# Three raw buffers for late weights, six buffers for reads of h, and the first pair's low parts of q and k on VectorE

## The chip, the cores and the metric

The kernel runs on one core of a Trainium2 chip. The time is what the device takes for one execution, in microseconds (us). A core has five engines that run their own instructions in a fixed order and meet at semaphores: TensorE (PE in the profile; PEld is its weight load), VectorE (DVE), ScalarE (ACT), GpSimd (POOL) and SyncE (SP). An engine that waits holds up everything behind it in its order. "SPq" and "ACTq" are the queues from which SP and ACT issue DMAs.

## What is computed

Three stages follow each other, all in float32:

```python
# attention with decay: q, k, v (4, 8, 576, 64), f (4, 8, 576)
cum = cumsum(log(clip(f, 1e-4, 1.0)))
scores = q @ k.T / 8 + cum[:, None] - cum[None, :]     # causal
x = softmax(scores) @ v                                # -> (2304, 512)
# first feed-forward: w_in (512, 2048), w_out (2048, 512)
h = x @ w_in
y = (h * tanh(softplus(h))) @ w_out                    # "Mish" of h
# second feed-forward: w1, w2, w3 (512, 768), w_out (768, 512)
out = max(y @ w1, y @ w2, y @ w3) @ w_out
```

## The kernel before

**Split operands.** Each float32 operand of a large product is split into a high part, which is the value rounded to the type that TensorE multiplies, and a low part, the rest. `split` does that with a copy and a subtraction, each on an engine that the caller names. `mm3` (L182 to L184) multiplies high by high, high by low and low by high: three matmuls for each product.

**Late weights.** The inputs' weights lie in HBM as 64-bit numbers. `load_f32` reads a chunk of them as raw pairs of 32-bit words (tile `wr`, L155) and builds the float32 value with five instructions: L160 (or L158 on ACT), L161, L164, L167 and L171, the rest on VectorE. Then `load_split` has the value split on two engines; for all late weights that is GpSimd twice (the copy at L139 and the subtraction at L143). "Late" are the weights that are loaded after attention: `load_w_out` (moe_w_out, 16 chunks of 512 columns, two raw buffers `wr`) and `load_w2` (24 chunks of 384 columns of w1, w2 and w3, then 6 chunks of 512 of the last w_out, one raw buffer `wr1`). The pool `stg2` holds the raw tiles and two buffers of the value `wt`.

**The stages in order.** Attention runs over 16 pairs of heads; `load` reads a pair's q, k, v and running sums, and `prep` splits and transposes them. The splits there are made by `split_raw`, the high part on VectorE and the low part on GpSimd. Between the pairs, `h_steps` computes `h` for blocks of 256 tokens; ACT or VectorE copies each result out of PSUM (tile `he`, L539 or L542) and a DMA writes it to HBM. What is left of the h steps after attention, "the tail of the h stage", runs from about 410 to 497 us, with `load_w_out` beside it.

Then comes the y stage, up to about 715 us. Its loop has one step for each pair of 128 rows of w_out and each block of 512 tokens (the last block has 256), 12 matmuls of 512 columns to a step. `load_g` reads h (tile `g`, L631), ACT applies Mish (L634) and makes the high part `gh` (L137), and VectorE subtracts to get the low part `gl` (L143). It is called three steps ahead, with four buffers each for `g`, `gh` and `gl`. Every second step also draws one chunk from `load_w2`. After the last step of a block the four results `y` are copied out of PSUM (tile `ze`, four buffers; L661 on VectorE, L664 on ACT) and written to HBM as `z_d`. The last stage (products `g` and `o`) reads them again as `yr`.

**What sets the order.** The order of each engine's instructions is written when the kernel is compiled, by a planner that simulates the engines and takes the ready instruction with the best priority. `tc.high_priority(AHEAD)` moves the reads and splits of h ahead of the rest. A tile with more buffers lets the planner put the next writer of that tile earlier.

Of the kernel before, what the change touches and what calls it, by code (L numbers as in the profile page):

```python
# [9 lines left out]
F32 = mybir.dt.float32  # L10
F32R = mybir.dt.float32r
BF16 = mybir.dt.bfloat16
I32 = mybir.dt.int32
# [18 lines left out]
AHEAD = 3000  # L32
BLK = 256
BLK2 = 512
# [33 lines left out]
def tile_decay_attention__mish_ff__max3_ff(  # L68
# [66 lines left out]
    def split(dst_hi, dst_lo, src, eng_hi, eng_lo):  # L135
        if eng_hi == "act":
            nc.scalar.activation(dst_hi, src, AF.Copy)  # L137
        elif eng_hi == "pool":
            nc.gpsimd.tensor_scalar(dst_hi, src, 1.0, 1.0, op0=ALU.mult, op1=ALU.mult)  # L139
        else:  # L140
            nc.vector.tensor_copy(dst_hi, src)
        eng = nc.gpsimd if eng_lo == "pool" else nc.vector
        eng.tensor_tensor(out=dst_lo, in0=src, in1=dst_hi, op=ALU.subtract)  # L143
# [3 lines left out]
    def load_f32(pool, srcs, bufs=None, abs_eng="dve", raw="wr"):  # L147

        m, n = len(srcs), srcs[0].shape[1]
        t = pool.tile([128, m, n], F32, name="wt", tag="wt", bufs=bufs)  # L150
        r = pool.tile([128, m, n, 2], I32, name=raw, tag=raw, bufs=bufs if raw == "wr" else 1)

        with tc.issue_after(pace[-1].ins) if pace else ExitStack():
            for i, src in enumerate(srcs):
                nc.sync.dma_start(r[:, i].rearrange("p n w -> p (n w)"), src.bitcast(I32))  # L155
        lo, hi, ti = r[:, :, :, 0], r[:, :, :, 1], t.bitcast(I32)
        if abs_eng == "act":
            nc.scalar.activation(t, hi.bitcast(F32), AF.Abs)  # L158
        else:
            nc.vector.tensor_scalar(ti, hi, 0x7FFFFFFF, None, op0=ALU.bitwise_and)  # L160
        nc.vector.tensor_scalar(  # L161
            t, t, F32_MIN_AS_HIGH_HALF, F32_MAX_AS_HIGH_HALF, op0=ALU.max, op1=ALU.min
        )
        nc.vector.tensor_scalar(  # L164
            ti, ti, 3, 0x3FFFFFF8, op0=ALU.logical_shift_left, op1=ALU.bitwise_and
        )
        nc.vector.scalar_tensor_tensor(  # L167
            out=ti, in0=hi, scalar=-0x40000000, in1=ti,
            op0=ALU.bitwise_and, op1=ALU.bitwise_or,
        )  # L170
        nc.vector.scalar_tensor_tensor(  # L171
            out=ti, in0=lo, scalar=29, in1=ti,
            op0=ALU.logical_shift_right, op1=ALU.bitwise_or,
        )
        return t
# [14 lines left out]
    wst = sa.enter_context(tc.tile_pool(name="wst", bufs=2))  # L190
# [55 lines left out]
    count = dict(pair=0, prep=0, unit=0)  # L246
# [20 lines left out]
                src[b, hs, 512:S, :].rearrange("h p d -> p h d"),  # L267
            )

    def split_raw(t, r, eng="dve"):  # L270

        split(t[:, :, 0], t[:, :, 1], r.rearrange("p (n d) -> p n d", d=64), eng, "pool")

    def load(b, hp):

# [33 lines left out]
    def prep(J):  # L309

        qh = as_.tile([128, 2, 512], F32R, name="qh", bufs=2)
        ql = as_.tile([128, 2, 512], F32R, name="ql", bufs=2)
        kk = as_.tile([128, 2, S], F32R, name="kT", bufs=2)
        last = q4[count["prep"] % 2]
        count["prep"] += 1

        def turn(dst, c, src):
            nc.tensor.transpose(dst[:, c:c + 128].bitcast(F32R), src, identr)

        rest = att_psum("tr")  # L320

        split_raw(qk[1], raw[1])
        split_raw(qk[0], raw[0])
        nc.gpsimd.tensor_scalar(
            qk[0][:, :, 2], raw[0].rearrange("p (n d) -> p n d", d=64), 1.0, 1.0, op0=ALU.mult, op1=ALU.mult
        )
        for i, part, dst, n in ((1, 0, kk, 0), (0, 0, qh, 1), (0, 1, ql, 2)):
            src = lambda blk: qk[i][:, blk, part:part + 2, :].rearrange("p a d -> p (a d)")
            for h in range(2):
                tr = att_psum("tr")  # L330
                for c in range(4):
                    turn(tr, c * 128, src(4 * h + c))
                nc.scalar.activation(
                    dst[:, h, 0:512].rearrange("p (c t) -> p c t", t=4),
                    tr.rearrange("p (t c) -> p c t", t=4),
                    AF.Copy,
                )
            turn(rest, n * 128, src(8))
        rr = rest[:, 0:384].rearrange("p (i h c) -> p i h c", i=3, h=2)
        nc.scalar.activation(kk[:, :, 512:S], rr[:, 0], AF.Copy)  # L340
        for a in range(2):
            nc.scalar.activation(
                last[:, a].rearrange("p (a c) -> p a c", c=64)[:, 0:4:3, :], rr[:, 1 + a], AF.Copy
            )
        split_raw(J["vs"], raw[2], "act")
        c2, c4 = J["cb"]
        for n, src, dst in ((2, 0, 5), (1, 3, 2), (1, 4, 4)):
            nc.gpsimd.affine_select(
                out=c2[:, :, dst:dst + n, :], in_=c2[:, :, src:src + n, :], pattern=[[0, 2], [0, n], [-1, 128]],
                compare_op=ALU.is_ge, fill=-1e30, base=0, channel_multiplier=1,  # L350
            )
        nc.gpsimd.tensor_tensor(out=c4[:, 512:S], in0=c4[:, 512:S], in1=mask4, op=ALU.add)
        J.update(q=(qh, ql), q4=last, k=kk)
# [222 lines left out]
    wo = [wop.tile([128, 2, 2, DM], F32R, name=f"wo{fp}") for fp in range(NFP)]  # L576
    stg2 = sb.enter_context(tc.tile_pool(name="stg2", bufs=2, side="right", reuse_waits="tile"))
    gp_ = sb.enter_context(tc.tile_pool(name="gp", bufs=4, side="right", reuse_waits="tile"))
    zst = sb.enter_context(tc.tile_pool(name="zst", bufs=4, side="right", reuse_waits="tile"))
    yps = sb.enter_context(tc.tile_pool(name="yps", bufs=5, space=PSUM, side="right", reuse_waits="tile"))  # L580

    def load_w_out():
# [23 lines left out]
    def load_w2():  # L606
        for c in range(KD):
            for m in range(3):
                src = (moe2_w1, moe2_w2, moe2_w3)[m][c * 128:(c + 1) * 128, :]
                for d in range(0, DFF2, 384):  # L610
                    ds = slice(d, d + 384)
                    load_split(
                        stg2, wm[m][:, 0, c:c + 1, ds], wm[m][:, 1, c:c + 1, ds], [src[:, ds]],
                        "pool", "pool", raw="wr1",
                    )
                    yield
        for c in range(NF2):
            load_split(
                stg2, wo2[:, 0, c:c + 1, :], wo2[:, 1, c:c + 1, :],
                [moe2_w_out[c * 128:(c + 1) * 128, :]], "pool", "pool", raw="wr1",  # L620
            )
            yield

    def load_g(ib, fp, a):

        g = gp_.tile([128, BLK2], F32, name="g")
        gh = gp_.tile([128, BLK2], F32R, name="gh")
        gl = gp_.tile([128, BLK2], F32R, name="gl")
        n = blocks1[ib][1]
        if n == BLK2:  # L630
            nc.sync.dma_start(g, h_d[ib][fp][:, a, :])  # L631
        else:
            nc.sync.dma_start(g.rearrange("p (a n) -> p a n", a=2), h_d[ib][fp][:])
        nc.scalar.activation(g, g, AF.Mish)  # L634
        split(gh, gl, g, "act", "dve")
        return [(t, (gh[:, i * n:(i + 1) * n], gl[:, i * n:(i + 1) * n])) for i, t in enumerate([a] if n == BLK2 else [0, 1])]

    wgen3 = load_w2()
    todo = [(ib, fp, a) for ib, (_, n) in enumerate(blocks1) for fp in range(NFP) for a in range(n // BLK)]
    with tc.high_priority(AHEAD):  # L640
        ahead = [load_g(*t) for t in todo[:3]]
    for step, (ib, fp, a) in enumerate(todo):
        n = blocks1[ib][1]
        if fp == 0 and a == 0:
            y = [yps.tile([128, n], F32, name=f"y{j}", tag="y") for j in range(KD)]
        parts = ahead.pop(0)
        if step + 3 < len(todo):
            with tc.high_priority(AHEAD):
                ahead.append(load_g(*todo[step + 3]))
        for t, g in parts:  # L650
            final = fp == NFP - 1 and t == 1
            for j in range(KD):
                js = slice(j * 128, (j + 1) * 128)
                mm3(y[j], (wo[fp][:, 0, t, js], wo[fp][:, 1, t, js]), g, fp == 0 and t == 0, final)
        if step % 2:
            next(wgen3, None)
        if final:
            for j in range(KD):
                ze = zst.tile([128, n], F32, name="ze", tag="ze")
                if j % 2:  # L660
                    nc.vector.tensor_copy(ze, y[j])  # L661
                    nc.sync.dma_start(z_d[ib][:, j, :], ze)
                else:
                    nc.scalar.activation(ze, y[j], AF.Copy)  # L664
                    nc.scalar.dma_start(z_d[ib][:, j, :], ze)
            if ib == 0:
                nc.sync.dma_start(y0[0], z_d[0][:, :, 0:BLK])
                split(y0[1], y0[2], y0[0], "act", "pool")
# [81 lines left out]
```

## Time and profile before

| what | value |
|---|---|
| median of 3 runs | 1026.43 us (1024.89 to 1028.39) |
| the profiled execution | 1024.48 us |
| its span, first to last instruction | 1022.5 us |
| mean granted TensorE clock | 0.968 |
| busy: PE, DVE, ACT, POOL | 955.2, 511.9, 422.0, 378.3 us |

The profile shows one execution. Busy time of PE includes matmuls that wait inside the engine, since their ends are modelled; counts of matmuls in a stretch of time tell more. A granted clock of 1.00 is 2.4 GHz, 0.5 is 1.2 GHz.

### The profile page before, as it was taken

How to read it: one execution, taken by the hardware profiler on the slowest of the kernel's cores; microseconds unless marked ns; L12 is line 12 of the kernel's file. 1: busy time of each engine (PE TensorE's matmuls, PEld its weight loads, DVE VectorE, ACT ScalarE, POOL GpSimd, SP SyncE). 2: the span in 40 equal slices, each digit the busy share in tenths (PEclk: the TensorE clock that was granted, in tenths of full speed). 3: DMA queues.
4: the chain of work that ended last, by engine and by line, in shares of the span. 5: the costliest groups of instructions: out<-in, count | busy, mean ns of one | idle time of the engine just before them, and what ended most of it. 6: DMA issues, size and time to landing. Idle time of an engine off the chain costs nothing.

```text
span 1022.5 us, 15879 instructions
## 1 busy us (share of the span) xinstructions
PE 955.2 (93%) x5756; PEld 840.6 (82%) x5756; DVE 511.9 (50%) x1159; ACT 422.0 (41%) x920; POOL 378.3 (37%) x437
## 2 busy tenths in 40 slices
PE   4886799999998999998898999999999999999998
PEld 4675689999998999998776777778988888888886
DVE  4868898656556556479645655653211112011110
ACT  4876667666667565421233434332211211211111
POOL 6756875566447521445423423230111111011110
PEclk9987789999999999999898999999999999999999
DMA  6545646545344412765445554552300100200101
GB/s 151 143 141 161 172 131 207 151 145 159 109 143 131 138 57 89 268 208 187 143 144 177 160 185 149 190 172 75 104 21 1 62 21 1 83 1 2 40 0 42
DMA packets 105294, 119.16 MB, mean 117 GB/s; under 512 B 33856, under 2 KB 77376, under 8 KB 105216
## 3 DMA queue, kind: packets, MB, share of 16 engines
q1 hardware_dynamic: 92288, 103.73, 33.0%
q10 hardware_dynamic: 12928, 14.42, 4.0%
q8 instruction: 45, 0.74, 0.3%
q14 instruction: 33, 0.27, 0.1%
HBM read 85.01 MB, written 33.10 MB: 116 GB/s over the span
## 4 chain that ended last, share of the span: by engine, by line
PE 57%; DMA 18%; DVE 17%; issue 2%; ACT 2%; SPq 2%; POOL 1%; DVEq 0%; ACTq 0%; POOLq 0%
PE g L183 7%; PE g L184 7%; PE g L182 7%; DMA wr<-in_moe_w_dram 7%; DMA wr<-in_moe_w_out_dram 5%; PE h L183 4%; PE h L184 4%; PE h L182 4%; PE av L451 4%; PE sc L363 4%; DVE wt L171 3%; PE pp L438 3%; DVE wt L167 3%; PE o L182 2%; PE o L184 2%; PE o L183 2%
## 5 line engine op out<-in xcount | busy, mean ns | idle before, releaser
L182 PE MATMUL h<-xh,wi 128*128 128x256 f32 x576 | 167.4, 292 | 8.2 <-ACT he L542 6.7
L183 PE MATMUL h<-xl,wi 128*128 128x256 f32 x576 | 167.1, 290 | 1.9 <-POOL xl L143 1.9
L184 PE MATMUL h<-xh,wi 128*128 128x256 f32 x576 | 166.2, 289 | 0.0
L143 POOL TENSOR_TENSOR hl<-mx,hh 128x512 fp32r<-128x512 f32 x27 | 36.5, 1350 | 271.3 <-ACT hh L137 271.3
L182 PE MATMUL g<-yh,wm 128*128 128x512 f32 (+1 forms) x360 | 134.5, 374 | 0.0
L183 PE MATMUL g<-yl,wm 128*128 128x512 f32 (+1 forms) x360 | 134.5, 374 | 0.0
L184 PE MATMUL g<-yh,wm 128*128 128x512 f32 (+1 forms) x360 | 134.5, 374 | 0.0
L183 PE MATMUL y<-gl,wo 128*128 128x512 f32 (+1 forms) x320 | 121.6, 380 | 10.5 <-DVE gl L143 10.5
L182 PE MATMUL y<-gh,wo 128*128 128x512 f32 (+1 forms) x320 | 120.5, 378 | 4.6 <-ACT gh L137 3.4
L182 PEld LDWEIGHTS h<-xh,wi 128*128 128x128 f32 x576 | 111.9, 195 | 9.5 <-ACT he L542 7.0
L184 PE MATMUL y<-gh,wo 128*128 128x512 f32 (+1 forms) x320 | 119.5, 375 | 0.0
L183 PEld LDWEIGHTS h<-xl,wi 128*128 128x128 f32 x576 | 111.9, 194 | 3.2 <-POOL xl L143 2.4
L184 PEld LDWEIGHTS h<-xh,wi 128*128 128x128 f32 x576 | 111.8, 194 | 0.3
L634 ACT ACTIVATE g<-g 128x512 f32<-128x512 f32 x72 | 45.5, 632 | 138.5 <-DMA g<-h_d 128.3
L706 DVE TENSOR_TENSOR mx<-g,mx 128x512 f32<-128x512 f32 x27 | 18.7, 691 | 158.6 <-PE g L184 158.6
L183 PEld LDWEIGHTS y<-gl,wo 128*128 128x128 f32 x320 | 61.8, 193 | 26.5 <-DVE gl L143 17.0
L414 ACT ACTIVATE P<-P,mn 128x128 f32<-128x128 f32 (+3 forms) x128 | 70.9, 556 | 27.3 <-DVE mn L408 26.4
L183 PEld LDWEIGHTS g<-yl,wm 128*128 128x128 f32 x360 | 68.2, 189 | 13.4
L184 PEld LDWEIGHTS g<-yh,wm 128*128 128x128 f32 x360 | 68.2, 189 | 13.2
L182 PEld LDWEIGHTS g<-yh,wm 128*128 128x128 f32 x360 | 68.1, 189 | 13.2
L182 PEld LDWEIGHTS y<-gh,wo 128*128 128x128 f32 x320 | 62.0, 194 | 17.3 <-ACT gh L137 4.9
L438 PE MATMUL pp<-ident,P 128*128 128x128 f32 x320 | 64.4, 303 | 11.9 <-POOL P L388 11.7
(101 smaller groups left out, 1989.9 us busy)
## 6 DMA issues: line engine op xcount, KB each, us to landing
g<-h_d SPq DMA_DIRECT2D x72, 256.0 KB, 3.3
h_d<-he ACTq DMA_DIRECT2D x46, 256.0 KB, 2.9
wr<-in_moe_w_out_dram SPq DMA_DIRECT2D x22, 512.0 KB, 4.0
wr<-in_moe_w_dram SPq DMA_DIRECT2D x24, 384.0 KB, 3.4
cb<-cum_d SPq DMA_DIRECT2D x64, 128.0 KB, 3.4
wr<-in_moe_w_in_dram SPq DMA_DIRECT2D x32, 256.0 KB, 3.3
h_d<-he SPq DMA_DIRECT2D x26, 256.0 KB, 3.2
cb<-cum_d SPq DMA_DIRECT2D x32, 144.0 KB, 3.3
```

Of the source, the lines that this page charges most:

```text
L143: eng.tensor_tensor(out=dst_lo, in0=src, in1=dst_hi, op=ALU.subtract)
L167: nc.vector.scalar_tensor_tensor(out=ti, in0=hi, scalar=-0x40000000, in1=ti, op0=ALU.bitwise_and, op1=ALU.bitwise_or,)
L171: nc.vector.scalar_tensor_tensor(out=ti, in0=lo, scalar=29, in1=ti, op0=ALU.logical_shift_right, op1=ALU.bitwise_or,)
L182: nc.tensor.matmul(ps, wh, xh, start=start, stop=False, skip_group_check=True)
L183: nc.tensor.matmul(ps, wh, xl, start=False, stop=False, skip_group_check=True)
L184: nc.tensor.matmul(ps, wl, xh, start=False, stop=stop, skip_group_check=True)
L363: nc.tensor.matmul(o, lhs, rhs, start=n == 0, stop=n == len(mms) - 1, skip_group_check=True)
L414: nc.scalar.activation(Pt, Pt, AF.Exp, scale=-1.0, bias=mn[:, col - 1:col], accum_out=sm[:, ci:ci + 1],)
L438: nc.tensor.transpose(pp[:, n * 128:n * 128 + 128], Pt[:, k0:k0 + 128], ident)
L451: nc.tensor.matmul(avp[h][:, off:off + w], vl, T[:, i, c:c + w], start=kt == 0 and i == 0 and not (g == 0 and h == 1), stop=last and i == ...
L634: nc.scalar.activation(g, g, AF.Mish)
L706: nc.vector.tensor_tensor(out=mx, in0=g[1], in1=mx, op=ALU.max)
```

## The change

The raw tile gets three buffers wherever the pool is not the early one (`wst`), and `load_w2` uses the same raw tile as `load_w_out`, so both share three buffers. `load_g` is cut in two: `load_g` reads h and applies Mish, five steps ahead and with six buffers; `split_g` makes the high and low parts, two steps ahead and with three buffers each. The tile `ze` goes from four buffers to three. In the first call of `prep`, the low parts of q and k are subtracted on VectorE and no longer on GpSimd.

```diff
-        r = pool.tile([128, m, n, 2], I32, name=raw, tag=raw, bufs=bufs if raw == "wr" else 1)
+        r = pool.tile([128, m, n, 2], I32, name=raw, tag=raw, bufs=3 if pool is not wst else bufs)
...
-    def split_raw(t, r, eng="dve"):
+    def split_raw(t, r, eng="dve", eng_lo="pool"):
-        split(t[:, :, 0], t[:, :, 1], r.rearrange("p (n d) -> p n d", d=64), eng, "pool")
+        split(t[:, :, 0], t[:, :, 1], r.rearrange("p (n d) -> p n d", d=64), eng, eng_lo)
...
-        split_raw(qk[1], raw[1])
-        split_raw(qk[0], raw[0])
+        first = "dve" if count["prep"] == 1 else "pool"
+        split_raw(qk[1], raw[1], "dve", first)
+        split_raw(qk[0], raw[0], "dve", first)
...
-    zst = sb.enter_context(tc.tile_pool(name="zst", bufs=4, side="right", reuse_waits="tile"))
+    zst = sb.enter_context(tc.tile_pool(name="zst", bufs=3, side="right", reuse_waits="tile"))
...
-                        "pool", "pool", raw="wr1",
+                        "pool", "pool",
...
-                [moe2_w_out[c * 128:(c + 1) * 128, :]], "pool", "pool", raw="wr1",
+                [moe2_w_out[c * 128:(c + 1) * 128, :]], "pool", "pool",
...
-        g = gp_.tile([128, BLK2], F32, name="g")
-        gh = gp_.tile([128, BLK2], F32R, name="gh")
-        gl = gp_.tile([128, BLK2], F32R, name="gl")
+        g = gp_.tile([128, BLK2], F32, name="g", bufs=6)
...
         nc.scalar.activation(g, g, AF.Mish)
+        return g, n, [a] if n == BLK2 else [0, 1]
+
+    def split_g(g, n, tiles):
+        gh = gp_.tile([128, BLK2], F32R, name="gh", bufs=3)
+        gl = gp_.tile([128, BLK2], F32R, name="gl", bufs=3)
         split(gh, gl, g, "act", "dve")
-        return [(t, (gh[:, i * n:(i + 1) * n], gl[:, i * n:(i + 1) * n])) for i, t in enumerate([a] if n == BLK2 else [0, 1])]
+        return [(t, (gh[:, i * n:(i + 1) * n], gl[:, i * n:(i + 1) * n])) for i, t in enumerate(tiles)]
...
-        ahead = [load_g(*t) for t in todo[:3]]
+        read = [load_g(*t) for t in todo[:5]]
+        ahead = [split_g(*read.pop(0)) for _ in range(2)]
...
-        if step + 3 < len(todo):
-            with tc.high_priority(AHEAD):
-                ahead.append(load_g(*todo[step + 3]))
+        with tc.high_priority(AHEAD):
+            if step + 5 < len(todo):
+                read.append(load_g(*todo[step + 5]))
+            if read:
+                ahead.append(split_g(*read.pop(0)))
```

## Rows read from the trace of the kernel before

**Rows 1.** Windows of the whole core; x counts instructions, PEclk is the granted clock.

```profile
core 0: us, PE busy (x) PEld busy (x) DVE busy (x) ACT busy (x) POOL busy (x), PEclk, DMA share, GB/s
480.00:490.00 10.00, 3.25 (x22) 3.05 (x21) 9.31 (x13) 1.71 (x3) 4.92 (x6) 0.85 0.47 165
490.00:500.00 10.00, 10.00 (x58) 9.43 (x58) 9.18 (x14) 1.83 (x3) 5.06 (x5) 0.81 0.41 133
500.00:690.00 190.00, 177.50 (x747) 140.24 (x746) 106.89 (x207) 71.17 (x124) 59.95 (x59) 0.97 0.51 165
620.00:630.00 10.00, 10.00 (x46) 8.23 (x45) 4.94 (x12) 4.26 (x8) 2.40 (x3) 1.00 0.42 144
```

**Rows 2.** Windows, instructions that touch y alone: PE, PEld, DVE and ACT busy.

```profile
500.00:690.00 190.00, 176.25 (x735) 138.19 (x734) 4.02 (x6) 3.47 (x6) 0.97 0.51 165
540.00:550.00 10.00, 8.02 (x22) 6.00 (x23) 1.37 (x2) 1.15 (x2) 0.66 0.66 202
590.00:600.00 10.00, 7.31 (x25) 5.28 (x26) 1.37 (x2) 1.16 (x2) 0.83 0.64 214
640.00:650.00 10.00, 7.75 (x31) 5.63 (x32) 1.28 (x2) 1.16 (x2) 1.00 0.67 223
```

**Rows 3.** Chain of waits, 500 to 520 us: start, length, what.

```profile
506.84 3.58 DMA wr<-in_moe_w_dram
...
513.35 3.77 DMA wr<-in_moe_w_dram
```

**Rows 4.** Groups by line, VectorE, 500 to 693 us: busy, mean ns, idle before.

```profile
L143 DVE TENSOR_TENSOR gl<-g,gh 128x512 fp32r<-128x512 f32 x60 | 45.3, 757 | 8.2 <-ACT gh L137 8.0
...
L160 DVE TENSOR_SCALAR wt<-wr 128x384 int32<-128x384 int32 x23 | 8.3, 360 | 57.0 <-DMA wr<-in_moe_w_dram 57.0
```

**Rows 5.** Windows, instructions that touch wt alone: DVE, ACT and POOL busy.

```profile
501.00:649.00 148.00, 49.91 (x115) 0.00 (x0) 44.13 (x46) 0.97 0.51 165
```

**Rows 6.** Waits, 430 to 500 us: total, times, longest.

```profile
DVE wt L160 <- DMA wr<-in_moe_w_out_dram: 6.9, 8, 3.6
PE h L182 <- ACT he L542: 6.7, 1, 6.7
```

**Rows 7.** Timelines of VectorE, SP's queue and ACT, 436 to 488 us: start, length.

```profile
436.23 0.69 DVE L143 TENSOR_TENSOR gl<-g,gh 128x512 fp32r<-128x512 f32 x1
...
483.79 0.68 DVE L143 TENSOR_TENSOR gl<-g,gh 128x512 fp32r<-128x512 f32 x1
...
484.50 0.33 SPq L631 DMA_DIRECT2D g<-h_d  x1
...
472.71 0.62 ACT L137 ACTIVATE gh<-g 128x512 fp32r<-128x512 f32 x1
...
487.29 0.63 ACT L634 ACTIVATE g<-g 128x512 f32<-128x512 f32 x1 [11.14 <-DMA g<-h_d]
```

**Rows 8.** Timelines of VectorE and GpSimd, 464 to 467 us.

```profile
465.02 1.39 DVE L161 TENSOR_SCALAR wt<-wt 128x512 f32<-128x512 f32 x1
466.44 0.43 DVE L164 TENSOR_SCALAR wt<-wt 128x512 int32<-128x512 int32 x1
...
464.08 0.62 POOL L139 TENSOR_SCALAR wo<-wt 128x512 fp32r<-128x512 f32 x1 [0.64 <-DVE wt L171]
464.79 1.34 POOL L143 TENSOR_TENSOR wo<-wt,wo 128x512 fp32r<-128x512 f32 x1
```

**Rows 9.** Timelines of VectorE and ACT with its queue, 543 to 548 us.

```profile
543.94 0.36 DVE L160 TENSOR_SCALAR wt<-wr 128x384 int32<-128x384 int32 x1 [3.52 <-DMA wr<-in_moe_w_dram]
...
547.14 0.68 DVE L661 COPY ze<-y 128x512 f32<-128x512 f32 x1
...
544.55 0.63 ACT L634 ACTIVATE g<-g 128x512 f32<-128x512 f32 x1 [1.41 <-DMA g<-h_d]
544.63 0.33 ACTq L665 DMA_DIRECT2D z_d<-ze  x1
```

**Rows 10.** Timelines of GpSimd and VectorE, 12 to 14 us.

```profile
12.24 0.64 POOL L348 TENSOR_SCALAR_AFFINE_SELECT cb<-cb 128x512 f32<-128x512 f32 x1 [0.24 <-DMA cb<-cum_d]
...
13.85 0.29 DVE L408 CUSTOM_DVE_ANT_0 P<-sc,cb 128x128 f32<-128x128 f32 x1 [4.85 <-PE sc L363]
```

## The prediction

> **What bounds the kernel now.** I started with the windows. From 500 to 690 us TensorE is busy for 177.5 of 190 us [rows 1], but a matmul that waits counts as busy, so I counted matmuls. In the stage that multiplies by the first output weights (PE groups y) an undisturbed window of 10 us holds 46 matmuls of 512 columns [rows 1], 0.217 us each; a step of the loop (12 matmuls) takes 2.61 us. There are 735 of them from 500 to 690 [rows 2], 159.8 us of work. The 12 others of TensorE's 747 are early ones of the last stage, 1.4 us. So 28.8 us are lost. The windows in which one block of tokens ends and the next begins hold 22, 25 and 31 [rows 2]: 5.2, 4.6 and 3.3 us lost, with the early ones taken off 11.7. The steady part lost 17.1.
>
> The chain of waits says why [rows 3]: a load of raw weights takes some 3.6 us, VectorE's five instructions on that chunk follow, and only then is the next load issued, since these weights have one raw buffer (wr1). The two loads shown start 6.5 us apart. From 500 to 693 us VectorE has 60 gl subtractions [rows 4] to the loops' 24 chunks of 384 columns and 6 of 512, so two gl, and two steps of TensorE, share a round of 6.5 us where they need 5.2. VectorE is idle for 57.0 us ahead of L160, ended by that load [rows 4], and the gl that TensorE needs stand behind this wait.
>
> Ahead of that lies the tail of the h stage. TensorE stood for 6.7 us, waiting for ACT's copy of h [rows 6]. The timeline shows ACT held 11.14 us by a Mish whose read of h was issued only at 484.50, behind gl at 483.79 [rows 7], although that gl's own high part had run at 472.71. The window from 480 holds 22 matmuls where 83 of the 256-column kind fit (0.12 us each): 7.4 us lost. The window from 490 has a granted clock of 0.81 [rows 1]: 3.8 us at the lower level (1.2 of 2.4 GHz) after TensorE had stood, half of it lost, 1.9. Together 9.3.
>
> **Raw buffers in the tail of the h stage.** Two become three. VectorE waited 6.9 us here for raw weights [rows 6], so gl comes up to 6 us sooner; of TensorE's 6.7 us some 0.7 stay, and the clock would hold. That could give 8. But VectorE is still behind its planned time when TensorE reaches the y stage, and the next gl are late there: I take 5.5 (bounds 0 and 9.3).
>
> **Raw buffers in the steady y stage.** One becomes three, so a load runs beside two other chunks and the 57.0 us go. What is late next is VectorE itself. Its 115 instructions on 23 chunks of 384 columns cover 49.91 us [rows 5], 2.17 a chunk, mostly with GpSimd's split of the chunk running in VectorE's idle time. Without that idle time they fall together, as they do in the h tail: there L161 took 1.39 us beside a GpSimd subtraction of 1.34, and L164 right after it, of the same size and kind, 0.43 [rows 8]. That adds 0.96 us to a chunk of 512 columns and, by columns, some 0.72 to one of 384. So a chunk is 2.89 us, or 3.85 for 512, and each step adds a gl of 0.69 [rows 7].
>
> How many chunks fall on a step? The engines' orders are written ahead, from expected times. Between the gl at 436.23 and that at 483.79 [rows 7] VectorE's order has 53 instructions on chunks, 10.6 chunks of 512. The second gl was expected right after its high part, at 472.71 + 0.62. The 37.1 us between, less 0.6 for a gl, make 3.44 us a planned chunk, by columns 2.58 for 384. A planned step of 2.61 us leaves 1.92 beside a gl, so without the wait a chunk falls on every 1.35 steps (1.8 for 512), and no longer on every second. VectorE is then late by 2.89 - 1.35 x 1.92 = 0.30 us a chunk, 0.39 for 512: 24 x 0.30 + 6 x 0.39 = 9.6 us lost, where 17.1 were; 7.5 gained. With s steps to every chunk the loss is 24 x 2.89 + 6 x 3.85 - 30 x 1.92s = 92.5 - 57.6s: nothing at s = 1.61 (17.1 gained), and 34.9 at s = 1 (17.8 slower). These are the bounds.
>
> The Trainium skill, page "SBUF — State Buffer", section "Who interferes with whom", has a rule for rows 8: VectorE and GpSimd share a pair of ports, locked for a whole instruction, and the later one stands. The trace agrees so far: L161 ended 0.28 us after GpSimd's subtraction. By the page GpSimd's high part could hold VectorE as well; what that would make is a rival below, worked out from rows.
>
> **Reads of h: six buffers, splits two ahead with three.** The read for step n+5 needs the buffer of step n-1, whose split is long done, so Mish seldom waits. Where blocks change, ACT's second copy of y stood behind a Mish (544.55) that had waited 1.41 us for its read, and VectorE's copies, the last at 547.14, behind a chunk that had waited 3.52 [rows 9]. Both waits go. The price: with three z buffers the fourth copy waits for the first one's write. That was issued at 544.63 [rows 9]; if it lands as late as a load (3.6 us), at 548.2, VectorE stands 1.1 us longer, with a gl behind it. Three split buffers instead of four leave a lead of two steps, 5.2 us, which covers that. I take half of the 11.7 us back, 6 (bounds 11.7 gained, 5 lost; the fourth change, after 690, is left at nothing).
>
> **First pair.** On VectorE each of the two subtractions takes 0.69 x 576/512 = 0.8 us, and GpSimd is rid of them, so the low parts come sooner. But the first reduce on VectorE, at 13.85, also needs its decay tile, ready at 12.24 + 0.64 = 12.88 [rows 10]: 0.9 us at most. Should k's subtraction go ahead of the scaling of the running sum, all reads of the decay are 0.8 late. The next pair's reads stand behind these in SP's order and don't move for q's sake. I take 0, with -0.9 and 0.8 as bounds.
>
> **Sum.** 5.5 + 7.5 + 6 = 19 us. The profiled execution took 1024.48, which is 1.95 below the median of three runs (1026.43): 1005.5 in its own terms, 1007.4 for the median, so 1007. About 0.3%, 3 us, is what a measurement of this kernel can tell from no change.
>
> **Rivals.** *VectorE has room enough*, with s at 1.61 or above. For it: VectorE is busy for only 106.9 of the 190 us [rows 1]. Then 17.1 + 9.3 + 6 = 32.4 go: 994. *Both GpSimd instructions of a chunk hold VectorE.* A chunk grows by the high part too, 0.62 us [rows 8], 0.47 by columns for 384: 24 x 0.77 + 6 x 1.01 = 24.5 lost in the steady part, 7.4 more than now, 1026.4 - 11.5 + 7.4 = 1022. Against: VectorE's instructions have gaps into which a high part fits. *SP's order keeps the loads apart*: raw loads stand in one queue with reads of h that wait for a gl [rows 7], three buffers never fill, and the edit does nothing: 1024 to 1027. Against: those reads now wait for an older gl. *The z buffer eats the block changes*, 5 lost and not 6 gained: 1018. *Slower: chunks crowd out gl.* The order puts a chunk into every step of the first half, and TensorE waits for gl behind weights that the last stage needs far later. With 11.5 gained elsewhere and 17.1 now, it decides where 92.5 - 57.6s passes 28.6, at s = 1.11; at s = 1 the time is 1026.4 - 11.5 + 17.8 = 1033. For it: the planner's s of 1.35 is not far off. Against: its own times bar it.
>
> **Chances.** Forecast (997 to 1017) 0.50; room enough 0.21; both hold 0.07; z buffer 0.08; loads kept apart 0.06; crowded out 0.08. Faster by over 0.3%: the first two, the z buffer and half of "both hold", 0.82. Same 0.10, slower 0.08. The range, 990 to 1021, leaves out "crowded out", "kept apart" and half of "both hold", 0.18.
>
> **What would show it.** VectorE's wait ahead of L160 falls from 57.0 us to under 15; L161 and L164 of 384 columns grow beyond 0.36 us; the last chunk of weights ends well ahead of 690; TensorE's wait for he shrinks below 2 us; windows of y hold 40 to 44 matmuls in the early blocks and 46 in the late ones. I would be wrong if the new order put another late read in front of ACT's copies of h, or if it reordered the attention stage, which the same planner orders and which is not priced here.

## The result and the profile after

The changed kernel takes 1019.45 us (median of 4, 1017.39 to 1020.86) beside 1026.04 for the kernel before on the same chip. The medians differ by 6.6 us. The ratio of the two kernels is put at 0.9917, with an interval of 0.9896 to 0.9938 that holds both: some 8.5 us faster. The forecast was 19 us. The profiled execution took 1018.71 us, with a span of 1016.9.

The windows of the whole core, with the columns of [rows 1]:

```profile
470.00:480.00 10.00, 5.45 (x33) 5.18 (x32) 9.76 (x14) 2.31 (x4) 5.29 (x5) 0.83 0.66 231
480.00:490.00 10.00, 10.00 (x84) 9.91 (x83) 9.73 (x15) 1.79 (x3) 5.46 (x6) 1.00 0.58 190
490.00:500.00 10.00, 10.00 (x82) 9.83 (x81) 9.72 (x14) 1.80 (x3) 5.29 (x6) 1.00 0.69 213
500.00:690.00 190.00, 179.51 (x774) 143.08 (x773) 131.87 (x212) 76.81 (x130) 57.29 (x60) 0.98 0.53 165
620.00:630.00 10.00, 10.00 (x45) 8.27 (x45) 2.77 (x4) 5.25 (x10) 0.00 (x0) 1.00 0.36 109
```

Those of instructions that touch y alone, as in [rows 2]:

```profile
500.00:690.00 190.00, 176.28 (x736) 138.29 (x737) 4.80 (x7) 4.10 (x7) 0.98 0.53 165
540.00:550.00 10.00, 7.15 (x18) 5.37 (x19) 1.37 (x2) 1.18 (x2) 0.66 0.79 249
590.00:600.00 10.00, 7.15 (x28) 4.48 (x26) 0.00 (x0) 1.16 (x2) 1.00 0.67 201
640.00:650.00 10.00, 9.27 (x40) 7.13 (x39) 1.38 (x2) 1.18 (x2) 1.00 0.52 181
```

VectorE went from 106.89 to 131.87 us of busy time between 500 and 690, and TensorE's y matmuls there from 735 to 736. So this stretch lost nearly what it lost before: 190 us, less 736 x 0.217 and 38 shorter matmuls at 0.117 (11 late ones of h, 27 early ones of the last stage), leave 25.9 us against 28.8. Where the loss lies has changed. The first two block changes hold 18 and 28 matmuls, the third 40.

VectorE's groups by line and shape, 500 to 693 us, answer to [rows 4]:

```profile
L143 DVE TENSOR_TENSOR gl<-g,gh 128x512 fp32r<-128x512 f32 x62 | 54.4, 878 | 55.6 <-ACT gh L137 55.6
L164 DVE TENSOR_SCALAR wt<-wt 128x384 int32<-128x384 int32 x23 | 13.2, 573 | 0.6
L160 DVE TENSOR_SCALAR wt<-wr 128x384 int32<-128x384 int32 x22 | 9.1, 415 | 0.9 <-POOL wm L143 0.9
L669 DVE COPY ze<-y 128x512 f32<-128x512 f32 x8 | 5.5, 686 | 2.0 <-DMA z_d<-ze 1.9
```

The 57.0 us of waiting for loads ahead of L160 are gone; the 0.9 left there are a wait for GpSimd. Their place is taken by VectorE itself: where the chain of waits held loads of weights [rows 3], it is now a row of VectorE's own instructions.

```profile
513.14 0.28 DVE wt L160
513.44 0.56 DVE wt L161
514.02 1.08 DVE wt L164
515.16 0.44 issue
515.60 0.68 DVE gl L143
516.56 0.47 DVE wt L171
```

The timelines of VectorE and GpSimd show why they are long, as [rows 8] did for the tail of h. The first two rows are VectorE's, the last two GpSimd's:

```profile
522.15 0.68 DVE L143 TENSOR_TENSOR gl<-g,gh 128x512 fp32r<-128x512 f32 x1
...
524.81 1.51 DVE L143 TENSOR_TENSOR gl<-g,gh 128x512 fp32r<-128x512 f32 x1
...
524.12 0.56 POOL L139 TENSOR_SCALAR wm<-wt 128x384 fp32r<-128x384 f32 x1 [2.11 <-DVE wt L171]
524.76 1.01 POOL L143 TENSOR_TENSOR wm<-wt,wm 128x384 fp32r<-128x384 f32 x1
```

Beside GpSimd's subtraction of 1.01 us the gl takes 1.51 us, without it 0.68. The next gl follow at 528.31 and 531.80, again 1.51 us long and with one chunk between two of them: a step takes VectorE 3.49 us where TensorE needs 2.61. The instructions on wt cover 77.66 us from 501 to 649 (142 of them), where [rows 5] had 49.91. VectorE has its last chunk instruction at 615.46; after that the windows of y hold 45 or 46 but for the block change.

The tail of the h stage, answering to [rows 6] and [rows 7]: waits, then the timelines of SP's queue, VectorE and ACT.

```profile
ACT g L634 <- DMA g<-h_d: 13.0, 3, 8.9
...
PE h L182 <- ACT he L544: 4.6, 1, 4.6
...
470.08 0.33 SPq L631 DMA_DIRECT2D g<-h_d  x1
...
468.95 1.10 DVE L143 TENSOR_TENSOR gl<-g,gh 128x512 fp32r<-128x512 f32 x1
...
461.30 0.62 ACT L137 ACTIVATE gh<-g 128x512 fp32r<-128x512 f32 x1
473.59 0.63 ACT L634 ACTIVATE g<-g 128x512 f32<-128x512 f32 x1 [8.86 <-DMA g<-h_d]
```

The late read is still there, 14 us earlier: issued at 470.08 behind the gl at 468.95, whose high part ran at 461.30. A Mish that waits for it holds ACT for 8.86 us. So the stall has only moved: the window from 470 now holds 33 matmuls, at a granted clock of 0.83, and those from 480 and 490 are full.

### The profile page after: what moved, and what is told of

It reads as the page before. It is cut to its first block, busy times and chain, and to the rows that moved or that the text cites. A ratio compares the mean times of both kernels' runs of the same rounds, so it can differ in the third digit from the quotient of the medians.

```text
span 1016.9 us, 15906 instructions
## 1 busy us (share of the span) xinstructions
PE 953.4 (94%) x5756; PEld 840.1 (83%) x5756; DVE 540.7 (53%) x1161; ACT 423.8 (42%) x920; POOL 371.9 (37%) x435
## 4 chain that ended last, share of the span: by engine, by line
PE 61%; DVE 11%; DMA 3%; issue 3%; POOL 1%; ACT 1%; ACTq 0%; POOLq 0%; DVEq 0%; SPq 0%
PE g L183 7%; PE g L184 7%; PE g L182 7%; PE h L183 4%; PE h L182 4%; PE h L184 4%; PE y L184 3%; PE y L183 3%; PE y L182 3%; PE sc L365 3%; PE av L453 3%; DVE wt L164 3%; PE o L182 3%; PE o L184 2%; PE o L183 2%
## 5 line engine op out<-in xcount | busy, mean ns | idle before, releaser
L184 PE MATMUL y<-gh,wo 128*128 128x512 f32 (+1 forms) x320 | 118.8, 372 | 0.0
L182 PEld LDWEIGHTS h<-xh,wi 128*128 128x128 f32 x576 | 110.4, 192 | 8.8 <-POOL wo L139 4.7
L184 PEld LDWEIGHTS h<-xh,wi 128*128 128x128 f32 x576 | 111.0, 193 | 0.5
L182 PE MATMUL y<-gh,wo 128*128 128x512 f32 (+1 forms) x320 | 107.5, 372 | 0.4 <-DVE ze L669 0.4
L143 DVE TENSOR_TENSOR gl<-g,gh 128x512 fp32r<-128x512 f32 x72 | 61.8, 858 | 66.8 <-ACT gh L137 66.8
L183 PEld LDWEIGHTS g<-yl,wm 128*128 128x128 f32 x360 | 67.9, 189 | 13.4
L184 PEld LDWEIGHTS g<-yh,wm 128*128 128x128 f32 x360 | 67.9, 189 | 13.4
```

The source lines that it names most:

```text
L182: nc.tensor.matmul(ps, wh, xh, start=start, stop=False, skip_group_check=True)
L183: nc.tensor.matmul(ps, wh, xl, start=False, stop=False, skip_group_check=True)
L184: nc.tensor.matmul(ps, wl, xh, start=False, stop=stop, skip_group_check=True)
```

## The experiments

One table for all. The columns av, h, y and o give the start, in us, of the last matmul of the attention, of h, of y and of the last stage in each profile; the last column is o less av, the time after the attention. Each ratio is to the kernel before on the same chip; its medians there were 1026.0 to 1027.8. Without both of the first pair's low parts on VectorE av lies between 407.6 and 412.0. This is a spread between executions: e1 and e6 give GpSimd and ScalarE the same order up to there, and differ by 2.3 us. The last column is free of it (598.1, 598.6 and 598.6 in e1, e6 and e8, whose medians agree as well).

| kernel | median us | ratio to before (95%) | av | h | y | o | o - av |
|---|---|---|---|---|---|---|---|
| before | 1026.04 | 1 | 410.7 | 497.0 | 716.4 | 1018.2 | 607.5 |
| changed | 1019.45 | 0.9917 (0.9896-0.9938) | 414.0 | 501.0 | 713.4 | 1012.7 | 598.7 |
| e1_pairs_alike | 1014.43 | 0.9881 (0.9868-0.9894) | 409.9 | 490.3 | 708.8 | 1008.0 | 598.1 |
| e2_first_pair_only | 1025.41 | 0.9981 (0.9965-0.9997) | 412.4 | 492.9 | 713.3 | 1015.1 | 602.7 |
| e3_raw_only | 1009.36 | 0.9829 (0.9812-0.9846) | 408.0 | 493.1 | 700.3 | 1002.1 | 594.1 |
| e4_reads_only | 1032.37 | 1.0055 (1.0036-1.0074) | 410.4 | 490.5 | 727.8 | 1027.4 | 617.0 |
| e5_splits_before_mish | 1012.07 | 0.9859 (0.9840-0.9877) | 410.5 | 489.0 | 706.4 | 1005.8 | 595.3 |
| e6_four_z_buffers | 1013.80 | 0.9872 (0.9854-0.9891) | 407.6 | 488.4 | 706.8 | 1006.2 | 598.6 |
| e7_third_split_back | 1010.80 | 0.9849 (0.9829-0.9870) | 412.0 | 492.0 | 704.8 | 1006.6 | 594.6 |
| e8_q_low_only | 1014.27 | 0.9877 (0.9855-0.9898) | 411.4 | 491.0 | 710.7 | 1010.0 | 598.6 |
| e9_mish_held | 1016.76 | 0.9906 (0.9888-0.9924) | 412.8 | 493.8 | 709.8 | 1009.1 | 596.3 |
| e10_raw_paced | 1001.93 | 0.9767 (0.9750-0.9784) | 410.2 | 495.8 | 696.3 | 998.1 | 587.9 |
| e11_raw_low_on_vector | 1002.02 | 0.9766 (0.9748-0.9783) | 409.1 | 494.1 | 691.9 | 993.7 | 584.6 |
| e12_raw_low_left_out | 1004.07 | 0.9791 (0.9772-0.9811) | 410.4 | 495.2 | 693.9 | 995.7 | 585.3 |
| e13_raw_two_splits | 1014.07 | 0.9859 (0.9838-0.9880) | 410.5 | 497.0 | 708.5 | 1007.9 | 597.4 |
| e14_raw_paced_low_on_vector | 996.26 | 0.9690 (0.9668-0.9711) | 410.0 | 495.1 | 689.8 | 991.6 | 581.6 |
| e15_and_mish_held | 990.66 | 0.9634 (0.9610-0.9657) | 411.6 | 489.0 | 684.9 | 986.7 | 575.1 |

### Which part does what

**e1_pairs_alike**: the changed kernel without the first-pair edit.

```diff
-        first = "dve" if count["prep"] == 1 else "pool"
+        first = "pool"
```

> The changed kernel with the first pair's low parts of q and k on GpSimd again. Theory: the first-pair edit made the attention stage 3 to 5 us longer (its last score matmul came 4.9 us later, its last product 3.3), so without it the time is 1014 to 1016 and the last score matmul is back near 394.4 us. Rival: the attention stage moved for another reason (the order as a whole was written anew because of the other edits); then the time stays at 1018 to 1020.

**e2_first_pair_only**: the kernel before with that edit alone.

> The kernel before with the first-pair edit alone. Theory: 3 to 5 us slower, 1029 to 1031, all of it ahead of 420 us. Rival: no change (1025 to 1027), since the first reduce comes only 0.4 us sooner and the next pair's reads don't move.

**e3_raw_only**: the kernel before with the raw buffers alone (the changed L151, and `load_w2` without its own raw tile).

> The kernel before with three raw buffers for the late weights alone (reads and splits of h, z buffers and the first pair as before). Theory: the raw buffers carry the gain of the y stage; the load waits of VectorE (72.7 us from 500 to 693) go, VectorE is full until the last chunk, and the time is 1018 to 1021. Rival: without the deeper reads of h, Mish waits longer and nothing is gained (1025 to 1027).

**e4_reads_only**: the kernel before with `load_g` cut in two, splits two ahead, reads five ahead and three z buffers.

> The kernel before with the reads of h five ahead in six buffers, splits two ahead in three and three z buffers, but the raw buffers as before. Theory: VectorE still waits some 72 us for raw weights, the y stage keeps its length, 1024 to 1028. Rival: the deeper reads carry the gain, since they clear the block changes: 1018 to 1021.

e1 came as its theory said, and e2 as its rival said. e3 and e4 fell outside both of their ranges: the raw buffers alone came 9 us under what was expected, the reads alone 4 us over.

By the ratios, of 1026 us: the raw buffers give 17.5 us; the reads cost 5.6 alone and, from e3 to e1, 5.3 in company; the first pair, from e1 to the changed kernel, costs 3.7 in company (5.0 by the medians) and gives 2 alone. 17.5 - 5.3 - 3.7 = 8.5, the result. So one part gives twice what is left, and the two others take half of it back.

### Why the reads cost: the third split

In e1 the seventh gl and those after it come 5 to 7 us after those of e3. The rows are SP's, ACT's and VectorE's of e1:

```profile
497.70 7.25 SPq L631 DMA_DIRECT2D g<-h_d  x3
...
500.81 0.63 ACT L634 ACTIVATE g<-g 128x512 f32<-128x512 f32 x1 [9.61 <-DMA g<-h_d]
501.34 1.13 ACT L137 ACTIVATE gh<-g 128x512 fp32r<-128x512 f32 x2
...
496.99 0.68 DVE L143 TENSOR_TENSOR gl<-g,gh 128x512 fp32r<-128x512 f32 x1
501.99 0.69 DVE L143 TENSOR_TENSOR gl<-g,gh 128x512 fp32r<-128x512 f32 x1 [4.31 <-ACT gh L137]
```

and VectorE's of e3:

```profile
495.44 0.93 DVE L143 TENSOR_TENSOR gl<-g,gh 128x512 fp32r<-128x512 f32 x1 [1.19 <-ACT gh L137]
498.16 0.69 DVE L143 TENSOR_TENSOR gl<-g,gh 128x512 fp32r<-128x512 f32 x1 [1.79 <-ACT gh L137]
```

The first row of e3 is the seventh gl, like the last of e1 (501.99). Two things meet in e1: one split less is in hand when the h stage ends (five gl have run by then, six in e3), and ACT's order has two high parts, ready, behind the Mish of a later tile whose read is late. e5, e7 and e13 take these apart; e6 tests the z buffers.

**e5_splits_before_mish**: e1, with the later Mish put behind the high part.

```diff
+        with tc.issue_after(last_hi[0].ins) if first_step else ExitStack():
+            nc.scalar.activation(g, g, AF.Mish)
```

> The changed kernel without its first-pair edit, and with ScalarE's order set by hand: in each step the high part of the tile two ahead goes ahead of the Mish of the tile five ahead (in the kernel without the first-pair edit the third and fourth high part after the h stage stood behind a Mish that waited 9.61 us for its read, and VectorE waited 4.31 us for them). Theory (the reads put a waiting Mish ahead of work that was ready): about 4 us come back, 1010.5 against 1014.43 for the kernel without the first-pair edit, and the sixth low part of the y stage starts near 498 us instead of 502. Rival (VectorE's sum of work sets the y stage whatever the start): within 1 us of 1014.4.

1012.07: 2.4 of the 4 us expected. The gl in question (the seventh, though the expectation calls it the sixth) starts at 497.72, as forecast, but from the next one on the lead is 2.2 us (four gl later 511.17 against 513.35).

**e6_four_z_buffers**: e1 with `bufs=4` for `zst`.

> The changed kernel without its first-pair edit, and with four z buffers as before. Theory (three z buffers hold the block changes: VectorE's copy of y waited 2.7 us in all for z writes): 1012, some 2.5 us under the 1014.43 of the kernel without the first-pair edit. Rival (the wait falls where VectorE has time by then): within 1 us of 1014.4.

1013.80, no difference: z buffers cost nothing that can be measured, though VectorE's copies wait 1.9 us for their writes in the changed kernel.

**e7_third_split_back**: e1 with gh and gl in four buffers, three splits ahead, reads four ahead in five buffers.

> The changed kernel without its first-pair edit, with splits three steps ahead again in four buffers each, and reads four steps ahead in five buffers. Theory (what was lost is the third split in hand when the h stage ends): 1009 to 1010.5, as with the raw buffers alone (1009.36). Rival (the reads' place in the queues of SyncE and ScalarE costs it): 1013 to 1015, no better than 1014.43.

1010.80, just above the range expected. After the attention it takes 594.6 us, as e3 does (594.1).

**e13_raw_two_splits**: e3 with gh and gl in three buffers and splits two ahead; the reads as before.

> The raw buffers alone, with the splits two steps ahead in three buffers each; the reads stay three steps ahead in four buffers, and four z buffers. Theory (what the reads' edit costs is the third split in hand, not the reads or z): 1013 to 1015, as far from the raw buffers alone (1009.36) as the kernel with the whole reads' edit (1014.43). Rival (the earlier reads in the queues cost part of it): 1010 to 1012.

1014.07, near e1, with nothing of the reads moved. So the third split is most of the loss: 3.1 us by the ratios, 4.7 by the medians, 3.3 after the attention, of 5.3, 5.1 and 4.0. The 2.2 us left by the ratios are within the interval of that difference, some 2.5 either way, so whether the reads' place in the queues costs anything is open; putting the high parts ahead of the Mish (e5) gave 2.3.

### What the first pair costs, and the order

**e8_q_low_only**: e1 with q's low part of the first pair on VectorE and k's on GpSimd.

> The changed kernel with only the first pair's low part of q on VectorE, that of k on GpSimd again; the order of the instructions stays that of the kernel without the first-pair edit but for some 15 places. Theory (the first-pair edit costs by the order that the planner then makes for GpSimd and SyncE at 18 to 40 us, not by its two instructions): 1013.4 to 1014.6, with the last product of the attention near 410 us. Rival (the two instructions on VectorE cost by themselves): 1016 or more, and half of the 4 us later attention.

1014.27, as e1. The orders hardly differ and nothing is lost: the edit of q's instruction is free. With both parts moved, the planner wrote another order for the pairs that follow. GpSimd and TensorE in the changed kernel:

```profile
35.85 0.64 POOL L350 TENSOR_SCALAR_AFFINE_SELECT cb<-cb 128x512 f32<-128x512 f32 x1 [1.83 <-DMA cb<-cum_d]
36.47 2.05 POOL L390 TENSOR_SCALAR P<-P,rr 128x384 f32<-128x384 f32 x4
...
37.11 0.55 PE L440 MATMUL pp<-ident,P 128*128 128x128 f32 x3 [2.57 <-POOL P L390]
41.88 0.46 PE L318 MATMUL tr<-identr,qk 128*128 128x128 f32 x4
```

and in e1:

```profile
32.52 2.05 POOL L390 TENSOR_SCALAR P<-P,rr 128x384 f32<-128x384 f32 x4 [0.39 <-DVE rr L387]
35.51 1.52 POOL L350 TENSOR_SCALAR_AFFINE_SELECT cb<-cb 128x512 f32<-128x512 f32 x3 [0.93 <-DMA cb<-cum_d]
...
33.16 0.55 PE L440 MATMUL pp<-ident,P 128*128 128x128 f32 x3 [0.54 <-POOL P L390]
37.09 0.46 PE L318 MATMUL tr<-identr,qk 128*128 128x128 f32 x4
```

The mask of the next pair's decay (L350) now stands ahead of the scaling of P (L390), and its DMA is late. The transposes of the next pair start 4.8 us later. At the end of the attention some 3 us are left of it: av is at 412.4 to 414.0 in the three kernels with the edit, and 410.2 on average in the others. The first reduce did gain, at 13.42 us instead of 13.85 [rows 10].

Two ends stay open. No run has both parts on VectorE in the old order, so that the order costs this, and not k's instruction, is read from these rows and not shown by a run. And e2 has the same rows, without being slower than the kernel before:

```profile
35.48 0.64 POOL L349 TENSOR_SCALAR_AFFINE_SELECT cb<-cb 128x512 f32<-128x512 f32 x1 [1.99 <-DMA cb<-cum_d]
36.10 2.05 POOL L389 TENSOR_SCALAR P<-P,rr 128x384 f32<-128x384 f32 x4
```

Its attention ends later too (412.4), but from there to the last h it takes 80.5 us where the kernel before takes 86.3. What the later attention costs may depend on what the new order does behind it; no run here separates the two.

### What bounds the y stage now

**e9_mish_held**: the changed kernel, with the Mish from the eleventh tile on behind ACT's last copy of h.

```diff
+        with tc.issue_after(last_he[0].ins) if (ib, fp, a) in todo[10:] else ExitStack():
+            nc.scalar.activation(g, g, AF.Mish)
```

> The changed kernel whole, with every Mish from the eleventh tile on put behind ScalarE's last copy of h, so that none of them stands ahead of a copy while it waits for its read (8.86 us in the changed kernel). Theory (from the end of the attention to about 610 us VectorE's sum of work sets the time, and TensorE's stall in the tail of h costs nothing): the last h product 8 to 10 us earlier, near 491, and the time within 1.5 us of the 1019.45 of the changed kernel. Rival (the prediction's: the stall in the tail of h is worth itself): 1011 to 1014.

h ends 7.2 us earlier, and the time falls by 2.7 us by the medians, 1.1 by the ratios and 2.4 after the attention. It lies between the two: the stall is mostly covered, not wholly. e1 and e13 say the same. Their waits of TensorE from 410 to 505 us, e1 first:

```profile
PE h L182 <- ACT he L544: 1.1, 1, 1.1
```

```profile
PE h L182 <- ACT he L544: 6.8, 1, 6.8
```

The longer stall of e13 does not show in its time, 1014.07 against 1014.43, though the two differ in the reads and z buffers as well.

**e10_raw_paced**: e3 with each chunk's VectorE instructions behind the low part split in its step.

```diff
         if step % 2:
-            next(wgen3, None)
+            with tc.issue_after(last_gl[0].ins):
+                next(wgen3, None)
```

> The raw buffers alone, with VectorE's instructions of each late chunk put behind the low part that the step before it splits, so that one chunk falls on two steps instead of one. Theory (with the loads always there VectorE takes a chunk on every step, 2.9 and 0.85 us beside the 2.62 us of TensorE, and idles after 610 us; spread out it fits): the y stage 5 to 10 us shorter, 1000 to 1005 against 1009.36 for the raw buffers alone. Rival (the number of chunks, not their place, sets VectorE's end): within 2 us of 1009.4, or later where the last chunks come after the y stage.

**e11_raw_low_on_vector**: e3 with `"pool", "dve"` in `load_w2`.

> The raw buffers alone, with the low parts of the late w1 to w3 and of the last w_out subtracted on VectorE instead of GpSimd: some 0.55 us more of VectorE's own work for a chunk of 384 columns. Theory (GpSimd's subtraction holds VectorE longer than VectorE would take for it: a chunk and a low part take 3.75 us together, against 2.8 from their shortest rows): 0.3 to 0.4 us saved a chunk, 1001 to 1006 against 1009.36. Rival (what lengthens VectorE's instructions is not that subtraction): 45 chunks of 0.55 us more, of which a third to a half tells: 1018 to 1022.

**e12_raw_low_left_out**: e3 with zeros for those low parts.

> The raw buffers alone, with GpSimd's subtraction of those late low parts replaced by writing zeros (the low parts of the late w1 to w3 and of the last w_out are left out of the result). Theory (the subtraction holds VectorE): the low part of a tile of h falls from 0.85 to about 0.7 us, a chunk of 384 columns from 2.9 to under 2.4, and the time to 995 to 1002. Rival (VectorE is slowed by something else, or only GpSimd's first copy holds it): the rows stay within 0.1 us and the time within 3 us of 1009.4.

For e10 and e11 the theories hold: 1001.93 and 1002.02. (e11's rival counts 45 chunks; `load_w2` has 30.) Leaving the subtraction out (e12) came to 1004.07, outside the 995 to 1002 expected, and its chunk to 2.50 us and not under 2.4. The price of the subtraction can be read from the rows by line, 500 to 600 us. First e3, then e12 (its L164 is e3's L161, its L167 e3's L164, its L170 e3's L167):

```profile
L143 DVE TENSOR_TENSOR gl<-g,gh 128x512 fp32r<-128x512 f32 x29 | 25.6, 884 | 1.1 <-ACT gh L137 1.1
L167 DVE SCALAR_TENSOR_TENSOR wt<-wr,wt 128x384 int32<-128x384 int32 x22 | 17.3, 786 | 0.4
L164 DVE TENSOR_SCALAR wt<-wt 128x384 int32<-128x384 int32 x22 | 12.7, 578 | 0.5
L161 DVE TENSOR_SCALAR wt<-wt 128x384 f32<-128x384 f32 x21 | 10.9, 517 | 0.2
```

```profile
L146 DVE TENSOR_TENSOR gl<-g,gh 128x512 fp32r<-128x512 f32 x33 | 25.2, 767 | 7.5 <-ACT gh L137 7.5
L170 DVE SCALAR_TENSOR_TENSOR wt<-wr,wt 128x384 int32<-128x384 int32 x22 | 13.0, 593 | 0.2
L167 DVE TENSOR_SCALAR wt<-wt 128x384 int32<-128x384 int32 x22 | 12.2, 553 | 0.2
L164 DVE TENSOR_SCALAR wt<-wt 128x384 f32<-128x384 f32 x21 | 8.2, 389 | 0.0
```

A round, that is a chunk of 384 columns and a gl summed over their six lines, takes 3.79 us in e3 and in the changed kernel alike, 3.26 in e12 and 3.62 in e11, where 0.60 of it is the subtraction itself. The shortest instances in e3 sum to 2.81. So a round is 0.53 us shorter without the subtraction on GpSimd. This price is a little low, since e12 writes zeros in its place; they wait for nothing, and GpSimd wrote most of them at once, beside VectorE's first rounds:

```profile
497.20 8.54 POOL L143 MEMSET wm<- 128x384 f32 x20
```

From 508 to 590 us, where only GpSimd's copy is left, the round takes 3.19 us in e12 and 3.83 in e3: 0.63 for the subtraction, and up to 0.4 for the copy. On VectorE the subtraction takes about as much (0.60), and the sum is smaller than with it on GpSimd, 3.62 against 3.79. The rest of e11's round, 3.05 from 508 to 590, is shorter than even the 3.19 of e12; why, no run here shows.

**e14_raw_paced_low_on_vector** has both edits, and **e15_and_mish_held** holds the Mish from the ninth tile on as well.

> The raw buffers alone, with the late chunks paced to one in two steps and their low parts on VectorE, the two edits that came to 1001.93 and 1002.02 one by one. Theory (both relieve VectorE between 500 and 610 us; with one of them it is still the bound there, with both TensorE is): 996 to 999. Rival (each alone has taken all that VectorE held): 1001 to 1003.

> As the paced kernel with the low parts on VectorE, and every Mish from the ninth tile on put behind ScalarE's last copy of h. Theory (with VectorE relieved, TensorE's stall of some 5 us in the tail of h is no longer covered by VectorE's sum): 3 to 5 us less than that kernel. Rival (it is still covered, as in the changed kernel, where the same edit gave 1 to 3 us): within 2 us of it.

996.26 and 990.66, 37 us under the kernel before. With VectorE relieved, holding the Mish, which gave 1 to 3 us before, gives 5.6, a little over the 3 to 5 expected. The windows of the whole core from 500 to 620 us, first the changed kernel and then e15:

```profile
500.00:620.00 120.00, 109.51 (x459) 84.94 (x458) 111.77 (x183) 43.50 (x75) 57.29 (x60) 0.97 0.62 194
```

```profile
500.00:620.00 120.00, 118.32 (x525) 97.35 (x524) 89.27 (x180) 51.87 (x92) 14.63 (x22) 1.00 0.61 192
```

## Why the prediction was right or wrong

The side was right, and 1019.45 lies in the range, but the forecast of 19 us was more than twice too high (8.5 by the ratio). **The step that failed is "Reads of h: six buffers, splits two ahead with three"**: 6 gained in the forecast, 5.3 lost on the chip, just past its own bound of 5. A second miss is the first pair, 0 against 3.7 lost, past its bound of 0.8. Without the two the forecast, 13 for the raw buffers, stands against 17.5, or 13.4 after the attention. Of these 13.4, by the table, 1.2 lie before the last h, where 5.5 were forecast, and 12.2 between it and the last y, where 7.5 were. The sum came near by luck.

**Reads of h.** "Three split buffers instead of four leave a lead of two steps, 5.2 us, which covers that" is the wrong sentence. It set the lead against a z write alone. But the lead is what TensorE lives on while VectorE runs at 3.5 us a step, and one split less cost 3.3 us (e13). The fear that was priced, the z buffer, was nothing (e6). The gain at the block changes did not come where it was expected either: the first two still hold 18 and 28 matmuls, for there VectorE is behind in any case. (With the chunks spread out, in e10, every window of 10 us from 500 to 570 holds 46, with a block change at 530.80 to 533.48 among them.) And the read "five steps ahead" does not come early in the order: in e1 SP issued three in a row from 497.70 on, and the Mish behind the first stood in front of high parts that were ready.

**First pair.** The two instructions took 0.74 and 0.76 us and the first reduce came 0.43 us earlier, as costed. The loss comes with the reorder of the attention, which the prediction named last as what would make it wrong and left unpriced; how far it is the order's alone is open, as said above.

**Raw buffers, tail of the h stage.** Forecast 5.5, and it did not come: in e3 TensorE still waits 5.1 us for he and in the changed kernel 4.6, since the read stands behind gl in the order and not behind a load; nor did the clock hold (0.83 from 470 to 480). And the stall was not worth itself: in the changed kernel VectorE is busy for 9.7 of 10 us from 470 to 500, and what sets the next gl is its sum (e9 against e15, e1 against e13).

**Raw buffers, steady y stage.** VectorE's price was right: 2.89 us a chunk forecast, 2.91 measured in e3. The steps per chunk were not: 1.35 forecast, 29 gl to 26 chunks or 1.12 in e3, and one to one at 524 to 535 in the changed kernel. By the prediction's own formula 1.12 would lose 92.5 - 57.6 x 1.12 = 28 us, more than the 17.1 of before, and the kernel would have been no faster. It is faster because the chunks end early (at 607 us in e3, 615 in the changed kernel), and nearly all that comes later runs at 45 or 46. The formula also adds the chunks' loss to that of the block changes and leaves out the splits in hand, while all three come out of the same lateness of VectorE; how much each is worth was not measured. So the forecast came near through two errors of opposite sign. The rival "chunks crowd out gl" had the mechanism and the wrong price.

**The other rivals.** "VectorE has room enough" is out for this order (111.77 of 120 us busy), but its condition was right: e10, with about 1.9 steps to a chunk (34 gl to 18 chunks from 500 to 600), is 7 us faster than e3. "Both GpSimd instructions hold VectorE" is partly so: of the 1.0 us by which a round is above its shortest rows, some 0.6 are the subtraction's, and the copy has a share of the rest (in e12 L167 takes 0.55 us at 520.55, beside the copy, and 0.35 at 523.33 without it). The Trainium skill, page "SBUF — State Buffer", section "Who interferes with whom", says that an instruction of VectorE with two inputs in SBUF contends with a GpSimd instruction that reads; gl at 1.51 us beside the subtraction and 0.68 without it agrees. "SP's order keeps the loads apart" is out (the 57.0 us of waiting for loads are gone), "the z buffer" too (e6).

**The signs named in advance.** The wait ahead of L160 fell below 15; L161 and L164 of 384 columns grew from 0.36 us to 0.43 and 0.57; the last chunk instruction came at 615.46; the late windows hold 45 or 46. Two did not come: TensorE's wait for he is 4.6 and not below 2, and early windows hold 18 to 38 beside some of 40 to 46, not 40 to 44 throughout. The first came in e1 (1.1), and brought nothing.

## What to carry to other kernels

Where a wait for a load goes, price the engine behind it as saturated. Sum its work per step, with what contends, and hold that against the work in hand: a buffer that looks spare can be the lead that carries the next engine over the dense stretch. If the saturated engine idles later, spread its work (here 7 us), or move onto it a helper's instruction that holds it up (here 7 us by itself, 13 with both). Only then look at stalls elsewhere, which it has been covering. And where a planner writes the orders, an edit of two instructions can be an edit of the whole order after them: compare the orders before pricing it at nothing.

## What was not expected of the hardware

VectorE was faster with GpSimd's subtraction added to its own work than with GpSimd doing it: 3.62 us (e11) against 3.79 (e3) for a chunk and a gl. The sum was 3.79 in the changed kernel and in e3, though the subtraction fell upon different instructions of VectorE: in the changed kernel gl was 1.04 us on average and L161 0.43, in e3 0.88 and 0.52.
